# Windowed attention, an MLP and a routed MLP in one kernel: transposes in another PSUM bank, a hundred matmuls over ones, one step of a weight conversion on another engine

## The chip, the cores and the metric

The kernel runs on one core of a Trainium2 chip. The metric is the device time of one execution in microseconds (us). Engines are named as the profile names them: PE (matrix multiplications), DVE (vector), ACT (scalar and activation functions), POOL (GpSimd), SP (whose queue issues the DMAs).

## What is computed

Three layers stand one behind the other. The inputs of the first two are in float64 or float32; the weights `w_in` and `w_out` of the second arrive as float64.

```python
# q, k, v: 4 x 8 heads x 576 x 64; window 128, causal, a linear bias per head
scores = q @ k.T / sqrt(64);  scores = where(mask, scores + bias, -1e9)
attn = softmax(scores);       x = (attn @ v)  as 2304 x 512
# MLP, 512 -> 2048 -> 512
h = x @ w_in;  x = (h - tanh(h)) @ w_out
# 8 experts, each token goes to one: cosine similarity, argmax, softmax gate
out[mask_e] = gate * (relu(x[mask_e] @ w1[e]) @ w2[e])
```

## The kernel before, in words

The 2304 rows are 18 blocks of 128. Attention of a block is done in four quarters of two heads (`quarter`). The MLP works on two blocks at a time in eight steps (`step`), 72 steps in all; a step multiplies two column blocks of `w_in` (L686, into `h`), forms h - tanh(h) on ACT (L691) and DVE (L694), splits it in a high and a low part (L699 on ACT, L703 on DVE, `gh` and `gl`) and multiplies by `w_out` (L710). The first 16 steps cover the first four blocks. Routing (`route`) and the experts come behind.

The two MLP matrices come as float64 pairs of 32-bit words and are turned into float32 pairs on the chip (`weight`), 16 pieces of `w_in` (`rawi`) and 16 of `w_out` (`rawo`), 512 KB each. Of each piece: the DMA (L298 or L300); the top three bits of the lower words (L325, on ACT); a scaled copy of the upper words (L307 on ACT or L309 on DVE, into one of three buffers `wst`); the sign merged in (L328, DVE); both merged (L331, DVE); the high part (L313, ACT or DVE); the low part (L317, mostly POOL). L328, L331 and L703 read two tiles of SBUF each.

The first four blocks take an early form of attention in float32. A quarter multiplies q and k of two heads (L456, `sc`), adds the bias and takes the extreme (L484, DVE), takes the exponential (L498, ACT, into `p` or `p32x`), transposes the exponentials on PE (L518), copies the transposes out (L524, ACT or DVE, into `ptf`) and multiplies by v (L535, into `of`). Each of the two heads has one tile `sc` in PSUM that holds the scores in its first half and the transposes of the exponentials in its second:

```python
self.scores = [self.psA.tile([128, 2, 2, 128], F32, tag=f"sc{n}", ...) for n in range(2)]
sc = v["sc"][jj] = self.scores[jj][:, 0]      # scores
t = self.scores[jj][:, 1]                     # transposes
```

A further bank, `misc`, serves small products: transposes of x for the MLP (L633), the router's products, the expert embeddings.

The order of all instructions is set by a planner (`Plan`): each task has the engines that may run it with a cost in us, a due time and the keys that it reads and writes; the planner places the task that can start earliest, the lower due time first, on the engine where it ends first. An engine then runs its list in that order, and an instruction whose input isn't there holds up all behind it on that engine. Moving one cost therefore moves many instructions.

Of the kernel before, what the change touches and what calls it, by code (L numbers as in the profile page):

```python
# [10 lines left out]
F32 = mybir.dt.float32  # L11
# [40 lines left out]
WRATE2 = 1.0  # L52
PAD = 8
# [109 lines left out]
class Builder:  # L163
# [15 lines left out]
    def setup(self):  # L179
# [35 lines left out]
        self.scores = [self.psA.tile([128, 2, 2, 128], F32, tag=f"sc{n}", name=f"sc{n}") for n in range(2)]  # L215
# [18 lines left out]

    def small(self):
        nc, i = self.nc, self.i
        nc.gpsimd.memset(self.ones, 1.0)
        nc.gpsimd.memset(self.half, 0.5)
        nc.gpsimd.memset(self.cum, 0.0)
        nc.gpsimd.memset(self.oh, 0.0)  # L240
        for j in range(self.NOV):
            nc.gpsimd.memset(self.thr[:, :, j:j + 1], float(128 * j))
# [43 lines left out]
    def weight(self, P, j, kind, f, due):  # L286
# [35 lines left out]
        if kind == "o" and 1 <= FT - f < NF:  # L322
            slots = [("kf", FT - f, 0), ("kf", FT - f, 1)]
        P.add({"SP": 1.46}, load, due - 2 - (EARLY if self.early() else 0), w=[raw, (raw, "L")] + slots)
        P.add({"ACT": 0.68}, lambda e: nc.scalar.activation(  # L325
            out=v["L"], in_=v["L"].bitcast(U32), func=AF.Copy, scale=7.499 * 2.0 ** -32), due, r=[raw], w=[(raw, "L")])
# [109 lines left out]
    def quarter(self, P, a, due):  # L436
# [13 lines left out]
        def scores(jj):  # L450
            sc = v["sc"][jj] = self.scores[jj][:, 0]
# [63 lines left out]
        def tr_pe(jj):  # L515
            t = self.scores[jj][:, 1]
            for x in range(W // 128):
                nc.tensor.transpose(t[:, x, :], v["p32"][:, jj * W + x * 128:jj * W + (x + 1) * 128], self.ident)  # L518

        def tr_out(e, jj):  # L520
            if jj == 0:
                v["pt"] = self.at.tile([128, 512], F32, tag=f"pt{a % 2}", name="ptf", bufs=1)
            t = self.scores[jj][:, 1].rearrange("p s t -> p (s t)")
            (nc.scalar.copy if e == "ACT" else nc.vector.tensor_copy)(  # L524
                out=v["pt"][:, jj * W:(jj + 1) * W], in_=t[:, 0:W])
# [55 lines left out]
        for jj in range(2):  # L581
            if early:
                P.add({"PE": 0.45 if one else 0.65}, lambda e, jj=jj: scores(jj), due,
# [582 lines left out]
    def build(self):  # L1166
# [10 lines left out]
        P.add({"POOL": 0.6}, lambda e: self.small(), 0, w=["small", "cum"])  # L1177
# [240 lines left out]
```

## Time and profile before

| | |
|---|---|
| Median of 3 runs (lowest, highest) | 847.39 us (847.25, 847.75) |
| The profiled execution | 849.56 us |
| Its span, first to last instruction | 847.8 us |
| Busy share PE, DVE, ACT, POOL | 96%, 67%, 52%, 30% |
| Instructions PE, DVE, ACT, POOL | 5244, 1500, 997, 246 |
| Granted TensorE clock, mean over the span | 0.996 |

The profiled execution is 1.76 us longer than its span and 2.17 us longer than the median of the runs. Busy shares are means over the whole; the change acts on the first 150 us, so the rows below are of stretches of that part. An engine is busy there while an instruction is executing, also when that instruction is held up inside by another engine. Idle times are put down to what ended last.

### The profile page before, as it was taken

To read this page: it belongs to the slowest core of one execution; us is meant where nothing else is said; L and a number is where in the kernel's file an instruction comes from. 1 tells how busy PE (TensorE), PEld (TensorE's weight loads), DVE (VectorE), ACT (ScalarE), POOL (GpSimd) and SP (SyncE) were. 2 spreads that over 40 slices of the span, in tenths; PEclk is the share of its full clock that TensorE was granted. 3 is DMA by queue.
4 is the path that set the end of the run, shared out by engine and by line. 5 is a ranking of instruction groups with operands and counts; after the bars stand their busy time and mean duration, and the time that the engine had idled before them with its cause. 6 is when DMAs were issued, how large, how long until landed. Compare 5 with 4: busy or idle time off the path is not lost.

```text
span 847.8 us, 15246 instructions
## 1 busy us (share of the span) xinstructions
PE 816.7 (96%) x5244; PEld 721.2 (85%) x5244; DVE 565.5 (67%) x1500; ACT 441.6 (52%) x997; POOL 252.1 (30%) x246
## 2 busy tenths in 40 slices
PE   6999999999999999999999999999999999999995
PEld 4677878988888899988998998989889899998994
DVE  4658999987778577777776775576366656666230
ACT  3759876665555355555554543464255545545120
POOL 1424676554424233324242240021110210111011
PEclk9999999999999999999999999999999999999998
DMA  8973325945334234433434312365266656555000
GB/s 299 334 268 121 109 94 160 270 107 130 96 82 135 40 82 106 87 87 91 99 83 102 80 41 48 125 212 162 84 198 216 216 166 189 193 163 174 20 27 30
DMA packets 109464, 112.88 MB, mean 133 GB/s; under 512 B 62901, under 2 KB 75189, under 8 KB 109248
## 3 DMA queue, kind: packets, MB, share of 16 engines
q1 hardware_dynamic: 106240, 102.35, 42.2%
q0 software_dynamic: 3136, 9.46, 3.0%
q8 instruction: 43, 0.70, 0.4%
q14 instruction: 45, 0.37, 0.1%
HBM read 87.12 MB, written 17.48 MB: 123 GB/s over the span
## 4 chain that ended last, share of the span: by engine, by line
PE 71%; DVE 11%; DMA 7%; issue 6%; ACT 2%; SPq 2%; POOL 1%; POOLq 0%; DVEq 0%; ACTq 0%
PE h L686 19%; PE acc L710 17%; PE he L1014 9%; PE y L1049 8%; PE o L546 3%; DMA pt<-ph 3%; PE sc L456 3%; PE sc L462 2%; DMA out<-yo,ix 2%; DVE wst L331 2%; PE y L1045 2%; PE misc L785 2%; PE of L535 2%; DVE rawo L328 1%; PE sc L518 1%
## 5 line engine op out<-in xcount | busy, mean ns | idle before, releaser
L686 PE MATMUL h<-xT,wi 128*128 128x256 f32 x1728 | 228.8, 287 | 0.0
L686 PEld LDWEIGHTS h<-xT,wi 128*128 128x128 f32 x1728 | 219.4, 193 | 6.4 <-issue 2.6
L710 PE MATMUL acc<-wo,gh 128*128 128x512 f32 x576 | 183.9, 400 | 0.0
L710 PE MATMUL acc<-wo,gl 128*128 128x512 f32 x288 | 112.9, 392 | 2.0 <-DVE gl L703 2.0
L710 PEld LDWEIGHTS acc<-wo,gh 128*128 128x128 f32 x576 | 99.7, 189 | 15.1 <-issue 0.7
L691 ACT ACTIVATE t<-h 128x512 f32<-128x512 f32 x72 | 43.1, 599 | 100.3 <-PE h L686 95.3
L1049 PE MATMUL y<-eo,ge 128*128 128x512 f32 x336 | 88.5, 399 | 0.0
L484 DVE CUSTOM_DVE_ANT_0 sc<-sc,bias 128x256 f32<-128x256 f32 (+1 forms) x144 | 52.7, 372 | 46.3 <-PE sc L462 29.4
L498 ACT ACTIVATE p<-sc,mx 128x256 f32<-128x256 f32 (+1 forms) x128 | 59.3, 464 | 34.1 <-DVE mx L484 26.0
L1074 POOL DMA_INDIRECT out<-yo,ix x24 | 23.4, 975 | 176.2 <-PE y L1045 61.0
L1049 PEld LDWEIGHTS y<-eo,ge 128*128 128x128 f32 x336 | 60.0, 188 | 9.7
L710 PEld LDWEIGHTS acc<-wo,gl 128*128 128x128 f32 x288 | 54.1, 188 | 15.1 <-DVE gl L703 2.9
L508 POOL TENSOR_TENSOR ph<-p,ph 128x512 f16<-128x512 f32 (+1 forms) x38 | 46.1, 1214 | 69.3 <-ACT ph L503 26.0
L703 DVE TENSOR_TENSOR gl<-t,gh 128x512 fp32r<-128x512 f32 x72 | 63.0, 876 | 4.6 <-ACT gh L699 4.4
L948 DVE TENSOR_TENSOR eo<-est,eo 128x512 fp32r<-128x512 f32 x60 | 45.0, 752 | 30.4 <-ACT eo L944 29.4
L1036 DVE SCALAR_TENSOR_TENSOR ge<-he,ge 128x256 fp32r<-128x256 f32 x104 | 29.9, 325 | 51.9 <-ACT ge L1030 51.9
L694 DVE TENSOR_TENSOR t<-h,t 128x512 f32<-128x512 f32 x72 | 49.5, 687 | 19.0 <-ACT t L691 19.0
L944 ACT CAST eo<-est 128x512 fp32r<-128x512 f32 x64 | 39.7, 620 | 40.1 <-PE y L1045 21.5
L1014 PE MATMUL he<-xT,ei 128*128 128x320 f32 x384 | 60.4, 309 | 0.0
L1014 PEld LDWEIGHTS he<-xT,ei 128*128 128x128 f32 x384 | 58.3, 188 | 2.3
L1030 ACT ACTIVATE ge<-he 128x320 fp32r<-128x320 f32 (+1 forms) x56 | 24.1, 430 | 67.5 <-PE he L1014 61.7
L1014 PE MATMUL he<-xA,ei 128*128 128x320 f32 (+1 forms) x384 | 59.0, 302 | 0.0
(181 smaller groups left out, 1425.6 us busy)
## 6 DMA issues: line engine op xcount, KB each, us to landing
est<-in_w SPq DMA_DIRECT2D x128, 256.0 KB, 2.9
rawi<-in_w_in SPq DMA_DIRECT2D x16, 512.0 KB, 6.6
rawo<-in_w_out SPq DMA_DIRECT2D x16, 512.0 KB, 7.3
stk<-in_k SPq DMA_DIRECT2D x30, 256.0 KB, 2.7
stq<-in_q SPq DMA_DIRECT2D x28, 256.0 KB, 2.8
bucket<-in_c_pad SPq DMA_DIRECT2D x8, 771.0 KB, 5.8
xe<-bucket SPq DMA_DIRECT2D x17, 257.0 KB, 3.5
vst<-in_v SPq DMA_DIRECT2D x30, 128.0 KB, 2.4
```

Source lines behind the costliest of these rows:

```text
L484: nc.vector.tensor_tensor_reduce(out=x, in0=x, in1=self.bias[:, h, c0:c1], scale=-0.125, scalar=mx[:, 1:2] if m else 3.0e38, op0=ALU.add, ...
L498: nc.scalar.activation(out=v["p32"][:, jj * W:(jj + 1) * W], in_=x, func=AF.Exp, scale=-1.0, bias=v["mx"][jj][:, 0:1], accum_out=self.sums ...
L508: self.eng(e).tensor_tensor(out=ph[:, 2 * W:4 * W], in0=v["p32"][:, 0:2 * W], in1=ph[:, 0:2 * W], op=ALU.subtract)
L686: nc.tensor.matmul(h3(v["h"], f2), lhsT=w[:, a, k, :], rhs=xT[c][:, :, k, :], start=(k == 0 and n == 0), stop=(k == KD - 1 and n == 2))
L691: nc.scalar.activation(out=v["t"], in_=v["h"].rearrange("p a b -> p (a b)"), func=AF.Tanh)
L694: nc.vector.tensor_tensor(out=v["t"], in0=v["h"].rearrange("p a b -> p (a b)"), in1=v["t"], op=ALU.subtract)
L703: self.eng(e).tensor_tensor(out=v["gl"], in0=v["t"], in1=v["gh"].bitcast(F32), op=ALU.subtract)
L710: nc.tensor.matmul(self.acc[g, t], lhsT=v[a][:, c0:c0 + 128], rhs=self.w["o", fs[f2]][:, c, :], start=(first and f2 == 0 and n == 0), stop ...
L944: nc.scalar.copy(out=t[:, 0, :], in_=v["x"])
L948: self.eng(eng).tensor_tensor(out=t[:, 1, :], in0=v["x"], in1=t[:, 0, :].bitcast(F32), op=ALU.subtract)
L1014: nc.tensor.matmul(h[:, 0:N], lhsT=w[:, a, c0:c0 + 128], rhs=xT()[b][:, k, 0:N], start=(k == 0 and n == 0), stop=(k == KD - 1 and n == 2))
L1049: nc.tensor.matmul(y[t], lhsT=gt(f, a)[:, (t - ts[0]) * 128:(t - ts[0] + 1) * 128], rhs=self.w["o", f0 + f][:, b, :], start=(f == 0 and n ...
```

## The change

Three edits. The exponentials of the early quarters are transposed into the bank `misc`, both heads at once, and copied out by one instruction instead of two; the score tiles keep only the scores. A hundred matmuls over a tile of ones (128x128 by 128x512, bfloat16, into the bank of `acc0`, read by nobody) are put into the plan with due time 0, nine with a cost of 0.43 us and the others with 0.215. The tile of ones is set first. The top bits of the lower words are formed by POOL (booked at 0.95 us) instead of ACT (0.68 us). The planner's costs for the early products of PE are lowered.

```diff
+NWARM = 100
-        self.scores = [self.psA.tile([128, 2, 2, 128], F32, tag=f"sc{n}", name=f"sc{n}") for n in range(2)]
+        self.scores = [self.psA.tile([128, 2, 128], F32, tag=f"sc{n}", name=f"sc{n}") for n in range(2)]
+    def warm(self, P):
+        nc = self.nc
+        at = {}
+        def mm(e):
+            if 0 not in at:
+                at[0] = self.psA.tile([128, 512], F32, tag="acc0", name="idle", bufs=1)
+            nc.tensor.matmul(at[0], lhsT=self.ones, rhs=self.ones.unsqueeze(1).to_broadcast([128, 4, 128]), start=True,
+                             stop=True)
+        for n in range(NWARM):
+            P.add({"PE": 0.43 if n < 9 else 0.215}, mm, 0, r=["ones"], w=[("acc", 0)])
...
-        P.add({"ACT": 0.68}, lambda e: nc.scalar.activation(
-            out=v["L"], in_=v["L"].bitcast(U32), func=AF.Copy, scale=7.499 * 2.0 ** -32), due, r=[raw], w=[(raw, "L")])
+        P.add({"POOL": 0.95}, lambda e: nc.gpsimd.tensor_scalar(
+            out=v["L"], in0=v["L"].bitcast(U32), scalar1=7.499 * 2.0 ** -32, scalar2=None, op0=ALU.mult), due, r=[raw],
+            w=[(raw, "L")])
...
-        def tr_pe(jj):
-            t = self.scores[jj][:, 1]
-            for x in range(W // 128):
-                nc.tensor.transpose(t[:, x, :], v["p32"][:, jj * W + x * 128:jj * W + (x + 1) * 128], self.ident)
+        def tr_pe(e):
+            v["tp"] = self.misc()
+            for x in range(2 * W // 128):
+                c = slice(x * 128, (x + 1) * 128)
+                nc.tensor.transpose(v["tp"][:, c], v["p32"][:, c], self.ident)
...
-                P.add({"PE": 0.45 if one else 0.65}, lambda e, jj=jj: scores(jj), due,
+                P.add({"PE": 0.3 if one else 0.42}, lambda e, jj=jj: scores(jj), due,
...
-            for jj in range(2):
-                P.add({"PE": 0.28 if one else 0.5}, lambda e, jj=jj: tr_pe(jj), due, r=["at", "con", ("p32", pb, jj)],
-                      w=[("tp", jj)])
-            for jj in range(2):
-                P.add({"ACT": 0.3, "DVE": 0.29} if one else {"ACT": 0.38, "DVE": 0.42}, lambda e, jj=jj: tr_out(e, jj),
...
-            P.add({"PE": 0.85 if one else 1.65}, pv_f, due,
+            P.add({"PE": 0.3 if one else 0.52}, tr_pe, due, r=["at", "con", ("p32", pb, 0), ("p32", pb, 1)], w=[("tp", a)],
+                  take="misc")
+            P.add({"ACT": 0.4, "DVE": 0.42} if one else {"ACT": 0.6, "DVE": 0.69}, tr_out, due, r=["at", ("tp", a)],
+                  w=[("pt", a % 2)], free="misc")
+            P.add({"PE": 0.45 if one else 0.9}, pv_f, due,
...
+        P.add({"POOL": 0.3}, lambda e: nc.gpsimd.memset(self.ones, 1.0), -30, w=["ones"])
+        self.warm(P)
```

What this does to the order on three engines. PE, at its start, before (`kf`, `qf` are k and q of the early blocks):

```order
L456 MATMUL sc_92<-kf_128,qf_126 128x128
L456 MATMUL sc_93<-kf_128,qf_126 128x128
L518 MATMUL sc_92<-con,p_160 128x128
L456 MATMUL sc_92<-kf_128,qf_126 128x128
L269 MATMUL misc<-con,ec 128x8 x4
L518 MATMUL sc_93<-con,p_160 128x128
L456 MATMUL sc_93<-kf_128,qf_126 128x128
```

and now, behind the first pair of scores:

```order
L471 MATMUL sc_92<-kf_131,qf_128 128x128
L244 LDWEIGHTS ones
L244 MATMUL idle<-ones 128x512
L283 MATMUL misc<-con,ec 128x8 x4
L471 MATMUL sc_93<-kf_131,qf_128 128x128
...
L534 MATMUL misc<-con,p_175 128x128 x2
L471 MATMUL sc_92<-kf_131,qf_128 128x128
```

Nine of the matmuls over ones stand ahead of the first scores and all hundred ahead of the first product of the MLP; behind it there is none. Of the 32 early score products 24 stand ahead of it now, 21 before.

DVE, in the early attention of block 1, with what each instruction waits for; before (L484 is the bias, L553 and L554 the sums' reciprocals):

```order
L484 ISA sc_92,mx_376<-sc_92,bias 128x256 [waits Activation_49]
L484 ISA mx_376 128x1
L331 SCALAR_TENSOR_TENSOR wst<-wst,rawo_275 128x512 [waits DVE_49]
L484 ISA sc_93,mx_391<-sc_93,bias 128x256 [waits Activation_49]
L484 ISA mx_391 128x1
L313 CAST wo_394<-wst 128x512 [waits DVE_49]
L328 SCALAR_TENSOR_TENSOR rawo_298<-rawo_298 128x512 [waits DMAHW1_49]
L553 TENSOR_SCALAR sm<-sm 128x4 [waits Activation_49]
```

and now:

```order
L343 SCALAR_TENSOR_TENSOR rawo_334<-rawo_334 128x512 [waits DMAHW0_49,Pool_49]
L343 SCALAR_TENSOR_TENSOR rawo_354<-rawo_354 128x512 [waits DMAHW1_49,Pool_49]
L566 TENSOR_SCALAR sm<-sm 128x4 [waits Activation_49]
L567 RECIPROCAL sm<-sm 128x4 [waits DVE_49]
L499 ISA sc_92,mx_470<-sc_92,bias 128x256 [waits PE_49]
L499 ISA mx_470 128x1
L499 ISA sc_93,mx_480<-sc_93,bias 128x256 [waits PE_49]
L499 ISA mx_480 128x1
L346 SCALAR_TENSOR_TENSOR wst<-wst,rawo_334 128x512
```

The bias instruction waited for ACT (its copy of the transposes out of the same tile) and now waits for the scores alone; the sign merge (L328, now L343) waits for POOL as well.

POOL, behind its constants, before:

```order
L362 TENSOR_TENSOR khl<-stk,khl 64x512 x2
L317 TENSOR_TENSOR wi_283<-wst,wi_283 128x512
L429 TENSOR_TENSOR vst_272<-vst_272,vt 128x256
L317 TENSOR_TENSOR wi_329<-wst_88,wi_329 128x512
L433 TENSOR_TENSOR vt<-vst_272,vt 128x4x64
L317 TENSOR_TENSOR wo_394<-wst,wo_394 128x512
```

and now:

```order
L339 TENSOR_SCALAR rawi_233<-rawi_233 128x512
L339 TENSOR_SCALAR rawi_247<-rawi_247 128x512
L339 TENSOR_SCALAR rawi_274<-rawi_274 128x512
L377 TENSOR_TENSOR khl<-stk,khl 64x512
L339 TENSOR_SCALAR rawi_294<-rawi_294 128x512
L444 TENSOR_TENSOR vst_318<-vst_318,vt 128x256
L339 TENSOR_SCALAR rawo_334<-rawo_334 128x512
```

The 32 new instructions (L339) lead on POOL: 7 of them stand ahead of the first low part (L317, now L331), 20 ahead of the eighth, 31 ahead of the sixteenth. Up to DVE's subtraction (L694, now L705) of the twelfth step DVE loses five high parts (L313), four scalings (L309), six copies of transposes (L524), two bias pairs and a few small ones to ACT or to a later place, and takes one `khl`.

## Rows read from the trace of the kernel before

**Rows 1.** Busy time by stretch: us, busy (x instructions) of each engine, PEclk, DMA share, GB/s.
```profile
0.00:20.00 20.00, 13.51 (x44) 9.10 (x44) 9.38 (x43) 7.34 (x23) 3.33 (x27) 1.00 0.89 295
20.00:66.00 46.00, 45.00 (x159) 32.75 (x158) 28.36 (x73) 30.11 (x80) 14.10 (x13) 1.00 0.86 305
66.00:90.10 24.10, 22.90 (x146) 17.78 (x146) 21.98 (x43) 20.39 (x51) 12.53 (x8) 1.00 0.34 112
90.10:150.10 60.00, 53.95 (x352) 48.11 (x352) 57.62 (x89) 44.71 (x88) 41.92 (x29) 1.00 0.41 128
150.10:847.80 697.70, 681.40 (x4549) 613.50 (x4547) 448.13 (x1256) 339.07 (x758) 180.19 (x171) 1.00 0.43 118
```

**Rows 2.** Timeline of PE: start us, us, line, operation, tiles, count [idle before].
```profile
5.46 0.80 PE L456 MATMUL sc<-kf,qf 64*128 64x128 f32 x4 [5.46 <-DMA kf<-in_k]
...
30.63 1.97 PE L535 MATMUL of<-vf,ptf 128*128 128x64 f32 x8 [0.58 <-DVE ptf L524]
...
50.08 2.93 PE L686 MATMUL h<-xT,wi 128*128 128x256 f32 x12
...
67.51 1.71 PE L686 MATMUL h<-xT,wi 128*128 128x256 f32 x12
69.06 1.00 PE L535 MATMUL of<-vf,ptf 128*128 128x64 f32 x8
...
88.38 0.62 PE L710 MATMUL acc<-wo,gh 128*128 128x512 f32 x2
88.84 0.40 PE L710 MATMUL acc<-wo,gl 128*128 128x512 f32 x1
89.07 0.62 PE L710 MATMUL acc<-wo,gh 128*128 128x512 f32 x2
```

**Rows 3.** Waits of DVE, 0 to 66 us: us in total, times, longest.
```profile
DVE sc L484 <- ACT ptf L524: 11.2, 11, 2.4
DVE ptf L524 <- PE sc L456: 5.8, 4, 1.9
```

**Rows 4.** Timeline of DVE, 108 to 113 us, and its twelfth L694.
```profile
108.44 0.68 DVE L331 SCALAR_TENSOR_TENSOR wst<-wst,rawi 128x512 int32<-128x512 int32 x1
...
110.69 1.79 DVE L331 SCALAR_TENSOR_TENSOR wst<-wst,rawo 128x512 int32<-128x512 int32 x1
112.40 1.78 DVE L703 TENSOR_TENSOR gl<-t,gh 128x512 fp32r<-128x512 f32 x1
...
150.12 0.69 DVE L694 TENSOR_TENSOR t<-h,t 128x512 f32<-128x512 f32 x1
```

**Rows 5.** Timeline of POOL over the same stretch.
```profile
110.18 3.46 POOL L317 TENSOR_TENSOR wi<-wst,wi 128x512 fp32r<-128x512 f32 x2
```

**Rows 6.** Groups of DVE by form, 66 to 150.1 us: busy us, mean ns | idle before.
```profile
L331 DVE SCALAR_TENSOR_TENSOR wst<-wst,rawo 128x512 int32<-128x512 int32 x13 | 14.6, 1128 | 0.0
L328 DVE SCALAR_TENSOR_TENSOR rawo<-rawo 128x512 int32<-128x512 int32 x12 | 13.1, 1110 | 0.0
L703 DVE TENSOR_TENSOR gl<-t,gh 128x512 fp32r<-128x512 f32 x10 | 12.0, 1204 | 0.0
L328 DVE SCALAR_TENSOR_TENSOR rawi<-rawi 128x512 int32<-128x512 int32 x9 | 9.8, 1101 | 0.0
L331 DVE SCALAR_TENSOR_TENSOR wst<-wst,rawi 128x512 int32<-128x512 int32 x11 | 8.8, 796 | 0.0
```

**Rows 7.** Groups of DVE by form, 0 to 66 us.
```profile
L328 DVE SCALAR_TENSOR_TENSOR rawo<-rawo 128x512 int32<-128x512 int32 x4 | 3.5, 872 | 0.0
L313 DVE CAST wi<-wst 128x512 fp32r<-128x512 f32 x2 | 1.5, 741 | 0.0
L524 DVE COPY ptf<-sc 128x128 f32<-128x128 f32 x4 | 1.2, 291 | 2.5 <-PE sc L456 2.2 <-ACT p32x L498 0.3
L313 DVE CAST wo<-wst 128x512 fp32r<-128x512 f32 x2 | 0.8, 418 | 0.0
```

**Rows 8.** The pieces of w_in, top bits on ACT: duration ns min/median/max, first and last start.
```profile
L325 ACT ACTIVATE rawi<-rawi x16: 649/680/717, 16.5 to 95.4; 128x512 int32<-128x512 uint32 x16
```

More of the change, by code (lines that the diff above doesn't have):

```diff
@@ L233, in consts @@
               r=[("xr", 0)], w=["tri"])
+    def warm(self, P):
[8 more added lines that the diff above has]
+            P.add({"PE": 0.43 if n < 9 else 0.215}, mm, 0, r=["ones"], w=[("acc", 0)])
     def small(self):
         nc, i = self.nc, self.i
-        nc.gpsimd.memset(self.ones, 1.0)
         nc.gpsimd.memset(self.half, 0.5)
@@ L450, in scores @@
         def scores(jj):
-            sc = v["sc"][jj] = self.scores[jj][:, 0]
+            sc = v["sc"][jj] = self.scores[jj]
             j = qq + 2 * jj
@@ L513, in tr, with tr_out @@
             nc.sync.dma_start_transpose(out=v["pt"][:, 0:4 * W // 128, :], in_=v["ph"][:, 0:4 * W])
-        def tr_pe(jj):
-            t = self.scores[jj][:, 1]
-            for x in range(W // 128):
-                nc.tensor.transpose(t[:, x, :], v["p32"][:, jj * W + x * 128:jj * W + (x + 1) * 128], self.ident)
[L520 to L525, printed above, removed]
+        def tr_pe(e):
[3 more added lines that the diff above has]
+                nc.tensor.transpose(v["tp"][:, c], v["p32"][:, c], self.ident)
+        def tr_out(e):
+            v["pt"] = self.at.tile([128, 512], F32, tag=f"pt{a % 2}", name="ptf", bufs=1)
+            (nc.scalar.copy if e == "ACT" else nc.vector.tensor_copy)(out=v["pt"][:, 0:2 * W], in_=v["tp"][:, 0:2 * W])
         def pv_f(e):
@@ L596, in quarter @@
         if early:
-            for jj in range(2):
-                P.add({"PE": 0.28 if one else 0.5}, lambda e, jj=jj: tr_pe(jj), due, r=["at", "con", ("p32", pb, jj)],
-                      w=[("tp", jj)])
-            for jj in range(2):
-                P.add({"ACT": 0.3, "DVE": 0.29} if one else {"ACT": 0.38, "DVE": 0.42}, lambda e, jj=jj: tr_out(e, jj),
-                      due, r=["at", ("tp", jj)], w=[("pt", a % 2, 1)] if jj else [("pt", a % 2), ("pt", a % 2, 1)])
-            P.add({"PE": 0.85 if one else 1.65}, pv_f, due,
-                  r=["at", ("pt", a % 2), ("pt", a % 2, 1)] + [("vf", x) for x in ([b] if one else [b - 1, b])], w=[("o", qq)] if qq else ["o", ("o", 0), ("o", 1)])
+            P.add({"PE": 0.3 if one else 0.52}, tr_pe, due, r=["at", "con", ("p32", pb, 0), ("p32", pb, 1)], w=[("tp", a)],
[3 more added lines that the diff above has]
+            P.add({"PE": 0.45 if one else 0.9}, pv_f, due,
+                  r=["at", ("pt", a % 2)] + [("vf", x) for x in ([b] if one else [b - 1, b])], w=[("o", qq)] if qq else ["o", ("o", 0), ("o", 1)])
             if qq:
@@ L1176, in build @@
         P = Plan()
-        P.add({"POOL": 0.6}, lambda e: self.small(), 0, w=["small", "cum"])
+        P.add({"POOL": 0.3}, lambda e: nc.gpsimd.memset(self.ones, 1.0), -30, w=["ones"])
+        self.warm(P)
+        P.add({"POOL": 0.6}, lambda e: self.small(), 0, r=["ones"], w=["small", "cum"])
         self.consts(P)
```

## The prediction, with its working

> **What bounds the kernel now.** I read the stretches first [rows 1]. From 150.1 us to the end PE is busy 681 of 698 us: whatever the first 150 us gain is kept there, and nothing in the change touches that part. So the question is how early the kernel reaches the state of 150.1 us, for which I take DVE's subtraction of the twelfth MLP step, at 150.12 us [rows 4]. The first 150 us fall in two. Up to 66 us PE is busy nearly throughout and DVE in 9.38 of 20 and 28.36 of 46 us; then DVE is busy in 21.98 of 24.1 and 57.62 of 60 us while PE idles 7.2 us in all [rows 1].
>
> The second view is PE's timeline [rows 2]. The same twelve matmuls of the MLP take 2.93 us at 50.08 and 1.71 at 67.51, the same eight of the attention 1.97 at 30.63 and 1.00 at 69.06. PE runs at 1.2 GHz up to about 66 us, although it is hardly ever idle, and at 2.4 GHz behind. The column of the granted clock says 1.00 for both stretches [rows 1] and doesn't tell the levels apart; the durations do.
>
> The third is DVE's waits up to 66 us [rows 3]: 11.2 us for ACT's copy of the transposes out of the score tile and 5.8 for the same copies on DVE itself behind PE. The fourth sets DVE beside POOL [rows 4, 5]: an L331 takes 0.68 us alone, and 1.79 while POOL is in two of its two-operand instructions, the L703 behind it 1.78. The two don't run beside each other; DVE stands until POOL is through, 1.1 us.
>
> **PE's account.** The attention and the first MLP products occupy PE for 13.51 + 45.00 = 58.5 us at the low clock [rows 1], half of it, 29.2, if the clock were high throughout; the first few us can't be, so I count 27. The 7.2 us of idle time behind 66 us could go too. Against that stand the hundred matmuls. At the high clock a 512-column product starts every 0.23 us (three between 88.38 and 89.07) [rows 2], at the low one I estimate twice that, 0.46. The nine ahead of the first scores take 4.1 us of the 5.46 that PE waits there anyway [rows 2]: nothing. The other 91 cost 20.9 us, all ahead of the first MLP product, where PE has no room otherwise if they come as planned: 44.6 us from 5.46 to 50.08 [rows 2] become some 22 + 21 = 43, so that product starts hardly earlier, but with three more score products done and at the high clock. PE's account thus gives at most 27 + 7.2 - 20.9 = 13.3 us.
>
> **DVE's account up to the twelfth subtraction.** First, what leaves: five L313 and four L309 at about 0.42 [rows 7], L309 taken alike, are 3.8 us, six copies 2.0 (0.29 to 0.42 each) [rows 7], two bias pairs about 1.0, and the small ones (a cast of ph, a reduction, four fills) about 1.6; with the 0.5 that two of the casts lost to POOL this makes 8.9. One `khl` is added, below 0.5 and left out.
>
> Second, POOL's 32 new instructions. None is in the trace. They are off DVE and cost it only where they hold up its two-operand instructions. From 66 to 150.1 us these stand above 0.68 us by 13 x 0.45 (L331 on rawo), 11 x 0.12 (on rawi), 12 x 0.43 and 9 x 0.42 (L328) and 10 x 0.52 (L703) [rows 6]: 21.3 us over POOL's 8 + 29 instructions [rows 1], 0.58 us each, where DVE is full. Up to 66 us the same excess is about 1.8 us (four L328 at 872 ns, two L313 at 741) [rows 7] over 14 such instructions of POOL: 0.13 each, where DVE has gaps. Twenty of the new ones stand ahead of POOL's eighth low part, which lay before 66 us, twelve behind it. That gives 20 x 0.13 + 12 x 0.58 = 9.6. DVE will have fewer gaps than now, so I take 12. The lower end is 5, if one operand keeps POOL half as long; the upper is 32 x 0.58 = 18.6.
>
> Third, DVE's idle time, 10.6 + 17.6 + 2.1 + 2.4 = 32.8 us now [rows 1]. The first 10.6 stay, since the first piece of w_in is there at 16.5 us in either case [rows 8]. Of the 17.6 the waits for the copies in the score tile go, DVE's own copies go with them [rows 3], and the scores come at the high clock, though spread by the matmuls over ones; I keep 7. Behind 66 us POOL's longer queue (a low part waits behind top bits, which wait for a DMA) lets me keep 3.4 of 4.5. Idle time falls to 21, by 11.8.
>
> The sum is -8.9 + 12 - 11.8 = **-8.7 us**, below PE's bound of 13.3, so DVE's account decides. ACT loses 32 instructions of 0.68 us [rows 8] and ten copies; it is busy in 65 of the 84 us behind 66 [rows 1] and holds nobody up for long, so that counts nothing by itself. Its freed time is what the nine casts and scalings use. The `misc` bank is held for one pair of transposes and one copy at a time, about 1.2 us per quarter against some 3.6 us per quarter on PE (43 us for twelve): covered. SP's order keeps its pieces, with four instead of two of w_in's near the end; they wait for slots of the early attention, which comes free earlier. 849.56 - 8.7 = 840.9 for the profiled execution, which stands 2.17 above the median: **838.7 us** in the median.
>
> **A rule that speaks against it.** The rows say that an L331 beside POOL takes 1.79 instead of 0.68 us [rows 4, 5]. The Trainium skill ("SBUF — State Buffer", section "Who interferes with whom") states it as an exclusive lock: a DVE instruction with two SBUF inputs and a GpSimd one exclude each other, and the second waits until the first is through. The trace agrees with its 1.1 us. By that rule alone, without gaps, each new POOL instruction could cost DVE its whole length, which is the slower rival below. The Trainium skill also says ("GPSIMD Engine Reference", section "4.1 Engine selection") that one-input operations run at about line rate there and two-input ones about twice as long; by it the second term would be nearer 5 and the result 832, which no row here shows.
>
> **The rivals.**
> *DVE stops being the bound (chance 0.18).* If the new POOL instructions are short and DVE's gaps close further, PE's account decides: 13.3 us less, 834.1. For it: the waits of [rows 3] lie just where PE was slow. Against: DVE's 57.62 of 60 us.
>
> *Nothing comes of it (0.10).* PE waits for DVE wherever it is faster, with the gaps before 66 us kept, because the matmuls over ones stretch a quarter to the old 3.6 us and so pace DVE as before. Then the idle term falls to about 0, and -8.9 + 9.6 is no change: 847 to 849.
>
> *POOL locks DVE out (0.08).* The wait per new instruction is that of the L703 beside POOL, 1.1 us [rows 4]. The second term is 32 x 1.1 = 35, the sum -8.9 + 35 - 11.8 = +14.5: 862. It turns to the slower side above (8.9 + 11.8) / 32 = 0.65 us per instruction, little more than the 0.58 that full stretches show. Against: 20 of the 32 stand where DVE has gaps.
>
> *The clock doesn't rise (0.05).* The change then does not do what it is for: the attention has kept PE busy for 58 us without the high clock coming. With short products between them the hundred might not do either, or the clock might fall again. The 91 then cost 41.9 us, the first MLP product starts at about 90 us, and the work that PE does now from 50.08 to 150.12 (100 us) follows in 85, without its 7.2 us of idle time and 8 us of the low clock: +25, 872. Against it: the clock rose at about 66 us, behind runs of twelve MLP products such as that at 50.08 [rows 2], and the products over ones are, like those, on full 128x128 weights. The Trainium skill ("TensorE: Matmul & The Clock Gate", section "What's actually happening") says that the throttled state is the default and activity releases it; this trace agrees for those MLP products and not for the 58 us of attention.
>
> **How the numbers follow.** The forecast has 0.58, the rivals 0.18, 0.10, 0.08 and 0.05; 0.01 is left for the unknown. The forecast's own range is from its second term: 5 gives 831.7, bounded by PE at 834.1, and 18.6 gives 845.3. The range for eight in ten takes in the first rival with some 2 us below it and the lower part of "nothing comes of it": 832 to 848. Within 0.2% (1.7 us, about what a measurement of this kernel can tell from no change) is the second rival, less a little on each side: 0.09. Faster: 0.58 + 0.18 and that little, 0.77. Slower: 0.08 + 0.05 and the rest, 0.14.
>
> **What the new profile would show.** Right: twelve MLP products at 1.7 us from the first on, attention products at half their old durations from about 8 us; the bias instruction on DVE waiting for scores alone; the excess of DVE's two-operand instructions grown by about 12 us up to the twelfth subtraction, and that one at 141 us instead of 150.1; new POOL instructions of 0.6 to 1.2 us; PE idle below 10 us between the first MLP product and 141 us. Wrong: products still at the low clock between 10 and 50 us; DVE idle in 20 to 50 us as before; L328 and L331 at 1.3 us or more on average; a stretch of waits on PE behind its first MLP product as long as what it saved.

## The result and the profile after

| | before | after |
|---|---|---|
| Median of 4 runs each on one chip (lowest, highest) | 847.57 us (847.25, 848.44) | 857.25 us (855.12, 858.0) |
| Ratio, 95% interval | | 1.0122 [1.0099, 1.0146] |
| Profiled execution, span | 849.56, 847.8 us | 858.0, 856.3 us |

The change makes the kernel 1.2% slower; 1.0% faster was forecast. Busy time by stretch after the change, with the cuts and columns of [rows 1]:

```profile
0.00:20.00 20.00, 17.98 (x88) 9.56 (x88) 10.50 (x43) 9.43 (x29) 6.07 (x29) 1.00 0.90 305
20.00:66.00 46.00, 40.47 (x237) 26.17 (x236) 30.12 (x67) 25.36 (x63) 43.22 (x30) 1.00 0.90 314
66.00:90.10 24.10, 20.50 (x114) 15.11 (x113) 16.39 (x36) 15.01 (x39) 22.96 (x17) 0.98 0.27 88
90.10:150.10 60.00, 56.72 (x364) 50.21 (x362) 54.84 (x80) 38.84 (x73) 48.16 (x32) 0.98 0.36 118
150.10:856.30 706.20, 684.46 (x4552) 615.60 (x4550) 452.67 (x1266) 339.12 (x760) 186.28 (x175) 0.99 0.43 118
```

POOL's column is the one that changed: 43.22 of 46 and 22.96 of 24.1 us, where it had 14.10 and 12.53 [rows 1]. From 20 to 90 us it is the busiest engine. Its two largest groups from 0 to 110 us (busy us, mean ns):

```profile
L339 POOL TENSOR_SCALAR rawo<-rawo 128x512 int32<-128x512 uint32 x16 | 28.0, 1751 | 1.8 <-DMA rawo<-in_w_out 0.6
L339 POOL TENSOR_SCALAR rawi<-rawi 128x512 int32<-128x512 uint32 x16 | 27.1, 1695 | 9.8 <-DMA rawi<-in_w_in 8.6
```

One of them in the view of the tile `rawi` after the change (duration ns min/median/max, first and last start):

```profile
L339 POOL TENSOR_SCALAR rawi<-rawi x16: 1549/1585/2076, 15.8 to 106.2; 128x512 int32<-128x512 uint32 x16
```

And the waits after the change, 0 to 110 us, those of ACT for POOL (us in total, times, longest):

```profile
ACT wst L321 <- POOL wi L331: 11.8, 6, 4.1
ACT wst L321 <- POOL wo L331: 9.8, 7, 2.9
...
ACT vt L446 <- POOL vst L444: 6.6, 3, 3.0
```

The 32 new instructions take 55.1 us of POOL. The planner had them at 0.95 us each, the prediction expected 0.6 to 1.2; none took less than 1.55. The low parts (L331) stand behind them in POOL's list, each holds one of the three buffers `wst`, and ACT's next scaling (L321) waits for that buffer 21.6 us. The chain of a weight thus runs at POOL's pace, ACT's freed time is spent waiting, and DVE gets its work late.

PE's timeline after the change (columns as in [rows 2]), at the start, at the first MLP products and at the 17th step:

```profile
1.11 3.48 PE L244 MATMUL idle<-ones 128*128 128x512 bf16 x9 [1.11 <-POOL half L252]
5.50 0.49 PE L471 MATMUL sc<-kf,qf 64*128 64x128 f32 x4 [0.91 <-DMA kf<-in_k]
...
31.52 1.00 PE L548 MATMUL of<-vf,ptf 128*128 128x64 f32 x8
...
60.60 3.21 PE L697 MATMUL h<-xT,wi 128*128 128x256 f32 x24
...
192.52 0.28 PE L697 MATMUL h<-xT,wi 128*128 128x256 f32 x1
194.74 4.51 PE L697 MATMUL h<-xT,wi 128*128 128x256 f32 x23 [1.94 <-DVE xT L657]
```

The high clock is there by 5.50 us: four score products take 0.49 us where they took 0.80 at 5.46, and eight attention products take 1.00 us at 31.52, where they took 1.97 at 30.63 [rows 2]. Yet the first MLP product starts at 60.60 us, 10.5 later than at 50.08 [rows 2]. At 194.74 PE has waited 1.94 us, and 23 products take 4.51 us, where 24 took 3.21 at 60.60: behind the wait PE is at 1.2 GHz again for a while. Here the granted clock shows it, with a mean of 0.63 from 194 to 198 us (columns as in [rows 1]):

```profile
194.00:198.00 4.00, 3.26 (x16) 3.26 (x17) 1.80 (x5) 0.57 (x2) 0.00 (x0) 0.63 1.29 254
```

To see where time goes I follow DVE's subtractions of the 72 MLP steps (L694 before, L705 after, as in [rows 4]), each against the same step before. The twelfth is at 150.06 us, so -0.1:

```profile
150.06 0.69 DVE L705 TENSOR_TENSOR t<-h,t 128x512 f32<-128x512 f32 x1
```

The 16th is at +1.5, the 17th at +8.9, the 36th at +6.2, the 72nd at +9.0. So the distance from the forecast has two parts: the 8.7 us that the first twelve steps were to gain did not come, and 7.4 us were lost in one step, the 17th. It is the first step of token blocks 4 and 5, whose attention, alone among those so far, goes through the transposing DMAs.

### The profile page after: what moved, and what is told of

The parts are those of the page before. It is cut to its first block, busy times and chain, and to the rows that moved or that the text cites. A ratio compares the mean times of both kernels' runs of the same rounds, so it can differ in the third digit from the quotient of the medians.

```text
span 856.3 us, 15453 instructions
## 1 busy us (share of the span) xinstructions
PE 820.1 (96%) x5344; PEld 716.7 (84%) x5344; DVE 564.5 (66%) x1486; ACT 427.8 (50%) x962; POOL 306.7 (36%) x279
## 4 chain that ended last, share of the span: by engine, by line
PE 62%; DMA 11%; POOL 9%; DVE 8%; issue 7%; ACT 2%; SPq 1%; POOLq 0%; DVEq 0%; ACTq 0%
PE h L697 16%; PE acc L721 14%; PE he L1025 10%; PE y L1060 8%; DMA pt<-ph 6%; PE o L559 3%; DMA out<-yo,ix 3%; POOL rawo L339 2%; PE y L1056 2%; PE sc L477 2%; POOL rawi L339 2%; PE misc L796 1%; POOL wo L331 1%; DVE wst L346 1%; POOL ph L523 1%
## 5 line engine op out<-in xcount | busy, mean ns | idle before, releaser
L697 PE MATMUL h<-xT,wi 128*128 128x256 f32 x1728 | 226.3, 285 | 3.5 <-DVE xT L657 1.9
L1060 PE MATMUL y<-eo,ge 128*128 128x512 f32 x336 | 88.5, 399 | 0.0
L714 DVE TENSOR_TENSOR gl<-t,gh 128x512 fp32r<-128x512 f32 x72 | 65.7, 913 | 13.2 <-ACT gh L710 13.0
L523 POOL TENSOR_TENSOR ph<-p,ph 128x512 f16<-128x512 f32 (+1 forms) x35 | 43.6, 1246 | 66.4 <-ACT ph L518 30.5
L705 DVE TENSOR_TENSOR t<-h,t 128x512 f32<-128x512 f32 x72 | 49.5, 687 | 18.0 <-ACT t L702 18.0
L1041 ACT ACTIVATE ge<-he 128x320 fp32r<-128x320 f32 (+1 forms) x56 | 24.1, 430 | 69.4 <-PE he L1025 64.0
```

The lines of the kernel that those rows point to most:

```text
L523: self.eng(e).tensor_tensor(out=ph[:, 2 * W:4 * W], in0=v["p32"][:, 0:2 * W], in1=ph[:, 0:2 * W], op=ALU.subtract)
L697: nc.tensor.matmul(h3(v["h"], f2), lhsT=w[:, a, k, :], rhs=xT[c][:, :, k, :], start=(k == 0 and n == 0), stop=(k == KD - 1 and n == 2))
L705: nc.vector.tensor_tensor(out=v["t"], in0=v["h"].rearrange("p a b -> p (a b)"), in1=v["t"], op=ALU.subtract)
L714: self.eng(e).tensor_tensor(out=v["gl"], in0=v["t"], in1=v["gh"].bitcast(F32), op=ALU.subtract)
L1060: nc.tensor.matmul(y[t], lhsT=gt(f, a)[:, (t - ts[0]) * 128:(t - ts[0] + 1) * 128], rhs=self.w["o", f0 + f][:, b, :], start=(f == 0 and n ...
```

## The experiments

In every row the columns "12th" to "72nd" are the start of that subtraction in the profiled execution minus its start before (150.12, 183.09, 191.71, 329.15 and 581.29 us). A median is compared only with the one of before in its own row; the ratio is the number to read for the time. The columns show where the time goes, in one execution of each kernel, and that execution is not always a typical one: before it took 849.56 us (medians 845.83 to 848.14), in e2 867.09 (864.07), in e12 856.48 (852.23), in e11 847.34, the fastest of four runs that reach up to 862.44. The change and e6, and e3 and e5, run the same instructions up to some 174 us and differ by 0.9 to 2.3 us at the twelfth and the 16th step. Smaller differences in these columns say nothing.

| | median, before (us) | ratio, 95% interval | 12th | 16th | 17th | 36th | 72nd |
|---|---|---|---|---|---|---|---|
| the change | 857.25, 847.57 | 1.0122 [1.0099, 1.0146] | -0.1 | +1.5 | +8.9 | +6.2 | +9.0 |
| e1_act | 846.66, 845.92 | 1.0000 [0.9986, 1.0015] | -8.9 | -7.5 | -2.2 | -3.4 | -1.1 |
| e2_pool_only | 864.07, 845.92 | 1.0213 [1.0188, 1.0238] | +18.6 | +18.1 | +16.2 | +18.0 | +17.9 |
| e3_half | 843.78, 845.92 | 0.9978 [0.9963, 0.9994] | -14.0 | -13.2 | -5.4 | -6.5 | -4.1 |
| e4_booked | 850.08, 845.92 | 1.0047 [1.0031, 1.0064] | +0.1 | +0.9 | -0.8 | +1.8 | +1.6 |
| e5_half_vt | 842.08, 847.14 | 0.9947 [0.9927, 0.9967] | -12.5 | -10.9 | -3.5 | -6.1 | -4.4 |
| e6_change_vt | 856.56, 847.14 | 1.0112 [1.0078, 1.0146] | -1.0 | -0.6 | +6.5 | +3.8 | +5.9 |
| e7_ones_only | 855.94, 847.14 | 1.0119 [1.0082, 1.0156] | +7.2 | +5.3 | +3.5 | +6.2 | +7.6 |
| e8_transposes_only | 848.33, 847.14 | 1.0016 [0.9986, 1.0045] | -5.5 | -5.8 | +3.8 | +0.3 | -0.9 |
| e9_half_lead1 | 843.85, 845.83 | 0.9970 [0.9951, 0.9989] | -10.7 | -11.4 | -9.7 | -7.5 | -4.6 |
| e10_half_lead2 | 842.63, 845.83 | 0.9952 [0.9935, 0.9970] | -10.5 | -9.1 | -11.3 | -8.7 | -5.8 |
| e11_half_lead4 | 852.72, 845.83 | 1.0118 [1.0047, 1.0190] | -0.8 | -5.6 | -7.7 | -3.3 | -1.8 |
| e12_before_lead2 | 852.23, 845.83 | 1.0076 [1.0051, 1.0100] | +7.6 | +7.7 | +6.3 | +8.3 | +7.4 |
| e13_change_lead2 | 855.09, 847.66 | 1.0104 [1.0074, 1.0134] | +1.0 | +3.0 | +0.8 | +3.6 | +5.4 |
| e14_act_lead2 | 846.42, 847.66 | 0.9991 [0.9973, 1.0009] | -1.5 | -4.6 | -6.1 | -3.9 | -2.5 |
| e15_either_lead2 | 843.38, 847.66 | 0.9970 [0.9950, 0.9990] | -10.9 | -11.2 | -12.4 | -6.9 | -6.2 |
| e16_quarter_lead2 | 839.75, 847.66 | 0.9916 [0.9886, 0.9947] | -13.7 | -11.9 | -14.1 | -11.8 | -9.1 |
| e17_quarter | 842.61, 848.14 | 0.9934 [0.9912, 0.9956] | -15.1 | -14.2 | -6.4 | -9.1 | -6.6 |
| e18_quarter_lead2_no_ones | 840.11, 848.14 | 0.9921 [0.9896, 0.9946] | -4.3 | -8.5 | -8.7 | -7.8 | -9.3 |

### Whose time POOL's new instructions cost

Three theories of the first part. *Occupancy*: POOL's own time is the bound. *Port*: POOL's instructions hold DVE up. *Order*: the plan, made with POOL at 0.95 us, is poor. **e1_act** takes the third edit back:

```diff
-        P.add({"POOL": 0.95}, lambda e: nc.gpsimd.tensor_scalar(
-            out=v["L"], in0=v["L"].bitcast(U32), scalar1=7.499 * 2.0 ** -32, scalar2=None, op0=ALU.mult), ...
+        P.add({"ACT": 0.68}, lambda e: nc.scalar.activation(
+            out=v["L"], in_=v["L"].bitcast(U32), func=AF.Copy, scale=7.499 * 2.0 ** -32), ...
```

> The change with the top bits back on ACT, all else kept (transposes in misc, the hundred matmuls). Occupancy theory (POOL is the bound from 20 to 110 us, because each new instruction takes 1.6 to 1.7 us and the low parts and the splits of k and q queue behind it): POOL busy below 70% in every 10 us up to 110, first MLP product at 50 us or earlier, 832 to 842 us. Matmuls theory (the hundred matmuls ahead of the first MLP product delay it): that product at 55 us or later and 850 us or more.

**e2_pool_only** makes the same edit the other way round, alone, in the kernel before.

> The kernel before with the top bits on POOL and nothing else. Occupancy theory: slower than before, 855 to 870 us, POOL busy above 90% from 20 to 110 us. Matmuls theory: the step alone is harmless, 845 to 850 us. Port theory (DVE held up by POOL): slower too, but then with the sign merge and the merge on DVE at 1.2 us or more on average; occupancy theory has them at about 0.9 to 1.1, as in the change.

**e3_half** keeps the change's plan and gives POOL half the columns, ACT the other half:

```diff
+        def top(e):
+            lo, up = v["L"][:, 0:256], v["L"][:, 256:512]
+            nc.gpsimd.tensor_scalar(out=lo, in0=lo.bitcast(U32), ...)
+            nc.scalar.activation(out=up, in_=up.bitcast(U32), ...)
+        P.add({"POOL": 0.95}, top, ...)
```

> The change with the same plan and order, but each top-bits instruction split: POOL does 256 of the 512 columns, ACT the other 256 at the same place of its list. Occupancy theory: POOL's part takes 0.8 to 0.9 us, POOL is relieved of some 27 us, 838 to 848 us. Matmuls theory: nothing changes, 855 to 858. Order theory (the plan books 0.95 us and is wrong by 0.7): with POOL's part near the booked time the order fits again, so 835 to 845, and the planner's booking of 1.6 in the next run does the same.

**e4_booked** only tells the planner the price: `P.add({"POOL": 1.6}, ...)` for 0.95.

> The change with POOL's top bits booked at 1.6 us instead of 0.95: the same work in an order that knows their length. Order theory: 838 to 846 us. Occupancy theory: POOL stays above 90% busy up to 110 us, whatever the order, 850 to 860 us.

The top bits on POOL alone cost 2.1% (e2), and without them the rest of the change is at the time of before (e1: 846.66 us, between the ranges of its two theories; its first MLP product starts at 53.2 us). With half the columns, in the change's own plan, the twelfth subtraction comes 14.0 us earlier than in the change (e3). POOL is still over 90% busy from 30 to 100 us there; what comes earlier is the work behind the new instructions: the 16th of the 32 low parts starts at 87.9 us in e3 and at 88.5 in e1, at 101.0 in the change and at 95.6 before. Booking the true price (e4) wins nothing at the twelfth step, though this is no clean test of the order, since the new plan gives DVE more to do (busy 125.0 us up to there, 111.8 in the change). But e4 loses nothing in the 17th step, and by its ratio it is 0.47% slower than before where the change is 1.22%. So occupancy decides the twelfth step; at the end the order weighs as much. For the port, first DVE's timeline in the change, 47 to 53 us:

```profile
47.81 0.69 DVE L346 SCALAR_TENSOR_TENSOR wst<-wst,rawi 128x512 int32<-128x512 int32 x1 [1.84 <-ACT wst L321]
...
50.42 0.69 DVE L343 SCALAR_TENSOR_TENSOR rawo<-rawo 128x512 int32<-128x512 int32 x1
51.75 0.69 DVE L346 SCALAR_TENSOR_TENSOR wst<-wst,rawo 128x512 int32<-128x512 int32 x1
52.35 0.69 DVE L343 SCALAR_TENSOR_TENSOR rawo<-rawo 128x512 int32<-128x512 int32 x1
```

and POOL's over the same stretch:

```profile
47.17 3.22 POOL L339 TENSOR_SCALAR rawi<-rawi 128x512 int32<-128x512 uint32 x2
50.48 3.98 POOL L339 TENSOR_SCALAR rawo<-rawo 128x512 int32<-128x512 uint32 x2
```

In this stretch DVE's two-operand instructions keep their 0.69 us beside L339, and POOL's pair is the one that grows, 3.98 for 3.22 us. In others DVE does wait for a part of an L339. DVE's timeline at 88 us:

```profile
88.07 1.13 DVE L346 SCALAR_TENSOR_TENSOR wst<-wst,rawi 128x512 int32<-128x512 int32 x1
...
89.74 1.14 DVE L346 SCALAR_TENSOR_TENSOR wst<-wst,rawi 128x512 int32<-128x512 int32 x1
```

and POOL's:

```profile
87.65 3.61 POOL L339 TENSOR_SCALAR rawo<-rawo 128x512 int32<-128x512 uint32 x2
```

Of the 24 instructions L343, L346 and L714 up to 150 us that meet L339 and nothing else on POOL, 14 take 0.68 to 0.69 us and ten 0.80 to 1.15; none waits for the whole of an L339. DVE's groups by form, 66 to 150.1 us after the change:

```profile
L343 DVE SCALAR_TENSOR_TENSOR rawo<-rawo 128x512 int32<-128x512 int32 x12 | 13.4, 1136 | 0.0
L346 DVE SCALAR_TENSOR_TENSOR wst<-wst,rawo 128x512 int32<-128x512 int32 x12 | 13.3, 1105 | 1.9 <-ACT wst L321 1.9
L714 DVE TENSOR_TENSOR gl<-t,gh 128x512 fp32r<-128x512 f32 x11 | 12.1, 1103 | 7.8 <-ACT gh L710 7.7
L346 DVE SCALAR_TENSOR_TENSOR wst<-wst,rawi 128x512 int32<-128x512 int32 x10 | 9.6, 957 | 0.0
...
L343 DVE SCALAR_TENSOR_TENSOR rawi<-rawi 128x512 int32<-128x512 int32 x6 | 7.4, 1260 | 0.0
```

1136, 1105 and 1103 ns stand where 1110, 1128 and 1204 stood, 957 and 1260 where 796 and 1101 stood [rows 6]. The time of all five above 0.68 us is 21.5 us, where it was 21.3; with the part up to 66 us it grows from 22.4 to 25.3 us. Hold-ups count as busy time, and the loss isn't there: up to the twelfth subtraction DVE is busy 111.8 us in the change and 114.2 in e1, and idle 38.3 and 27.0. The port theory falls as the cause; some 3 us of DVE's time are what it explains.

### The other two edits

**e7_ones_only** puts `self.warm(P)` with its tile of ones into the kernel before.

> The kernel before with the hundred matmuls over ones alone: its exponentials go through the DMA as before and ACT keeps the top bits. DVE's account: DVE is the engine that bounds the first 110 us and loses no work here, so a faster clock buys little: 844 to 848 us. PE's account: the cold products of the first 40 us cost more than the fillers, and the time is 836 to 842 us. The fillers run in front of products that are due: 850 us or more.

**e8_transposes_only** is e1_act without `self.warm(P)`.

> The change without matmuls over ones and with the top bits back on ACT: the early exponentials go through PE's transposes into the small products' bank, on a cold PE in the first 40 us. DVE's account: 8.9 us of DVE's work are gone whatever the clock, so the 12th subtraction comes 5 to 9 us early as in e1_act, and the end at 844 to 848 us. PE's account: the transposes and the single float products at half clock add what the 27 us of the prediction's sum say, and the time is 852 us or more.

The fillers (the hundred matmuls) alone cost 1.2%, the worst of the three expectations. (In this kernel the early exponentials go through PE, L518, and not through the DMA as that text says.) The first MLP product starts at 67.0 us (50.08 before), and DVE is busy 131.2 us up to the twelfth subtraction, 13.8 more than before; by what chain was not followed. The transposes alone come out like e1, at the time of before (e8's runs lie between 842.21 and 852.63 us), though both are 5 to 9 us ahead at the twelfth step. Both lose that lead again: e8 9.6 us in the 17th step, e1 5.3 us there.

### The 17th step

In the change and in e3 one instruction stands out at that place. DVE's timeline in the change:

```profile
189.26 3.39 DVE L448 TENSOR_TENSOR vt<-vst,vt 128x256 bf16<-128x256 f32 x1
...
194.00 0.69 DVE L657 TENSOR_TENSOR xT<-misc,xT 128x512 fp32r<-128x512 f32 x1
```

and POOL's beside it:

```profile
189.38 0.63 POOL L585 TENSOR_TENSOR xr<-xr,sm 128x256 f32<-128x256 f32 x1
189.96 1.28 POOL L385 TENSOR_TENSOR qst<-stq,qst 128x512 fp32r<-128x512 f32 x1
191.20 1.16 POOL L523 TENSOR_TENSOR ph<-p,ph 128x512 f16<-128x512 f32 x1
```

DVE stands 3 us beside three of POOL's two-operand instructions, and the residual's split (L657), for which PE waits, comes behind. I took this meeting for the cause. **e5_half_vt** and **e6_change_vt** give that one instruction to POOL, in e3's kernel and in the change:

```diff
+        def low(e):
+            if e == "DVE" and not self.moved:
+                self.moved, e = True, "POOL"
+            self.eng(e).tensor_tensor(out=v[2], in0=st["v"], in1=v[1], op=ALU.subtract)
```

> The kernel of e3_half with one instruction on another engine, in the same place of the program: the first lower part of v that DVE subtracts (128x256, 3.39 us at 174.75 us in e3_half, where DVE's thirteen others take a median of 0.42) goes to POOL. Lockout theory: that one instruction stands still while POOL runs three two-operand instructions end to end (174.88 to 177.85); behind it wait the residual's split for the next products (PE idle 1.95 us) and on SP the load into its buffer with two transposing DMAs behind it (PE idle 1.86 us), and after these pauses 60 products run at half clock: 7 to 8 us in all. Without it step 17 keeps the 13 us gained at step 16, and the time is 836 to 838.5 us. Order theory: the later blocks' attention lags by the plan, whoever subtracts this part; the waits come back some microseconds later, and the time is 842 to 845 us.

> The change itself with that same one instruction on POOL (3.39 us at 189.26 us there). Lockout theory: the loss between the 16th and the 17th subtraction (+1.5 to +8.9 us against the kernel before) goes, and the time is 848.5 to 851 us. Order theory: 856 to 858 us. If POOL's load of the first 110 us and this one meeting are the whole loss, this and e3_half add up: change minus 14 minus 7.

Both miss: the 17th step still loses 7.4 and 7.1 us. What took the place of the 3.39 us, in DVE's timeline of e5:

```profile
177.96 2.92 DVE L575 TENSOR_SCALAR sm<-sm 128x4 f32<-128x4 f32 x1 [0.32 <-POOL xr L594]
```

and in POOL's:

```profile
177.25 0.63 POOL L594 TENSOR_TENSOR xr<-xr,sm 128x256 f32<-128x256 f32 x1
177.82 0.68 POOL L456 TENSOR_TENSOR vt<-vst,vt 128x256 bf16<-128x256 f32 x1
178.45 1.28 POOL L388 TENSOR_TENSOR qst<-stq,qst 128x512 fp32r<-128x512 f32 x1
179.70 1.15 POOL L532 TENSOR_TENSOR ph<-p,ph 128x512 f16<-128x512 f32 x1
```

Now an instruction over 128x4 numbers stands until POOL's run ends at 180.85 us. So moving one instruction leaves DVE's stop where it was. Why is this step late in most of these kernels? The attention of blocks 4 and 5 gets its due times from the plan. PE's first product of it with v, before:

```profile
139.41 0.73 PE L546 MATMUL o<-vt,pt 128*128 128x192 bf16 x8
```

and in the change:

```profile
149.48 0.73 PE L559 MATMUL o<-vt,pt 128*128 128x192 bf16 x8
```

In e1 it starts at 138.3 and in e3 at 135.5 us: 1.1 and 3.9 us earlier than before, where the MLP's products are 9 and 14 us ahead. (This is not the first product of that attention, as the expectation of e9 has it: single scores stand earlier, from 113.3 us before, 100.3 in the change, 82.1 in e1 and 87.9 in e3.) **e9**, **e10** and **e11** have it due 1, 2 and 4 steps earlier in e3's kernel, **e12** 2 steps earlier in the kernel before, **e13** in the change:

```diff
-                d0 = p - 8 * rate - LEAD + 4 * n * rate
+                d0 = p - 8 * rate - (LEAD + 2 if g == 2 else LEAD) + 4 * n * rate
```

> The kernel of e3_half with the attention of token blocks 4 and 5 (the first that goes through the transposing DMAs, and the first products of which are step 17) due one step earlier in the plan. Second-bound theory: in every kernel so far the 17th subtraction stands at 186 to 201 us, 7 to 18 us behind the 16th where the first half was faster, since the planned attention of these blocks begins at 135 to 149 us whatever the products gained; due a step (some 7 us) earlier, PE waits less for the residual there and the time is 838 to 841 us. Total-work theory: VectorE and the other engines have no room for it before, the products of steps 9 to 16 come later by as much, and the time stays at 842.5 to 845 us.

> The same, due two steps earlier. Second-bound theory: no wait is left at step 17, 13 us gained there stay to the end but for a few: 836 to 839 us. Total-work theory: 842 to 846 us.

> The same, due four steps earlier. Second-bound theory: no better than two steps, since the wait at step 17 is gone by then, and the attention now stands in front of weights that the first twelve steps need: 838 to 844 us. Total-work theory: 846 us or more.

> The kernel before with the attention of blocks 4 and 5 due two steps earlier: a control. Second-bound theory: PE waits under 1 us between steps 16 and 17 of the kernel before, so there is nothing to win: 845 to 849 us, and what e10_half_lead2 wins over e3_half comes from the change. If it wins as much here as there, the plan was poor in itself and the change has nothing to do with that part.

> The change itself with the attention of blocks 4 and 5 due two steps earlier. Second-bound theory: the loss between steps 16 and 17 (+1.5 to +8.9 us) goes and POOL's load up to step 12 stays: 849 to 852 us. POOL theory for that loss too (POOL's backlog from the top bits delays the splits that this attention needs, so that a due time changes nothing): 856 to 860 us.

In e9 1.7 us of the loss in the 17th step are left, in the others with an earlier due time none: e13 stands at +0.8 behind +3.0, where the change has +8.9 behind +1.5. PE's timeline there, in e13:

```profile
188.83 3.03 PE L697 MATMUL h<-xT,wi 128*128 128x256 f32 x24
```

The 24 products come without a wait and at the high clock. That the late attention is the cause of this step's loss is shown. The end moves less: against e3, e9 and e10 keep 0.5 and 1.7 us of it at the 72nd subtraction, against the change e13 keeps 3.6, and the intervals of the ratios overlap in both comparisons. Steps 9 to 16 pay a part (e10 has -9.1 at the 16th, e3 -13.2), four steps are too many (e11), and in the kernel before the same edit costs 0.8%, all of it by the twelfth step (e12, which misses its 845 to 849 us). Second bound is right about the 17th step; the times of e9, e10 and e11 lie where total work had them, and that of e13, 855.09 us, between its two ranges.

### What is left of the change

**e14_act_lead2** is e1_act with that due time, **e15_either_lead2** the change with it and `P.add({"ACT": 0.68, "POOL": 1.6}, top, ...)`, **e16_quarter_lead2** is e10 with columns 0 to 127 on POOL and the others on ACT, **e17_quarter** is e16 with the old due time, **e18_quarter_lead2_no_ones** is e16 without `self.warm(P)`.

> The change with its top bits on ACT (e1_act) and the same attention two steps earlier. If the prediction failed only in POOL's price and in taking the gain of the first 150 us for kept, this is the kernel that it forecast: 838 to 842 us. If ACT's 0.68 us for each of the 64 (the part that the prediction took for free on ACT) or DVE's load before step 12 bounds it, 844 to 848 us.

> The change with the planner free to give each of the top bits' instructions to ACT at 0.68 or to POOL at 1.6 us, and the attention two steps earlier. Occupancy theory: some go to POOL where it idles, and neither engine is the bound: 838 to 842 us. If it does no better than e10_half_lead2 (842.6), the choice by instruction is worth nothing over the split by columns.

> The kernel of e10_half_lead2 with 128 of the 512 columns on POOL and 384 on ACT. Occupancy theory: POOL's 32 instructions are shorter still (1.08 us at 256 columns), ACT's longer; if POOL still bounds the first 66 us, 840 to 842 us; if ACT, whose part runs beside it, has become the bound, 843 to 845 us.

> The change with 128 of 512 columns on POOL and 384 on ACT, its attention due as in the change. Both bounds matter: a little better than e3_half (0.9978) and worse than e16 (0.9916): ratio 0.994 to 0.997, with a loss of 5 us or more between steps 16 and 17. If the due time is worth nothing, the ratio is 0.990 to 0.993.

> The kernel of e16 without the hundred matmuls over ones. PE's account: the transposes and single float products run at half clock until PE's clock rises by itself, and the first 60 us lose more than the ones took: ratio 0.997 to 1.003. DVE's account: DVE and the weights' arrival set the first 66 us, the ones are worth nothing: ratio 0.990 to 0.994.

e14 misses the forecast's range and lies in the other, 844 to 848 us (the top bits are 32 instructions, not the 64 of that text): its twelfth step is at -1.5, and DVE is busy in 57.33 of the 60 us from 90.1 (busy time by stretch, columns as in [rows 1]):

```profile
90.10:150.10 60.00, 55.85 (x375) 49.68 (x374) 57.33 (x102) 44.25 (x93) 41.42 (x29) 1.00 0.50 128
```

With the top bits on ACT, DVE is nearly full there as it was before, and earlier attention takes room from the weights. e15, where the planner puts 19 of the 32 on POOL, does no better than e10 (0.9970, 0.9952): a choice by instruction is worth nothing over the split by columns. e16 is the fastest kernel here, 0.8% below before and, by the two ratios, 2% below the change. e17 lies between e3 and e16, with 7.8 us lost in the 17th step where e16 loses none: the intervals of e16 and e17 overlap, so what the due time gives at the end is not settled. POOL's groups in e16 for its quarter (busy us, mean ns):

```profile
L341 POOL TENSOR_SCALAR rawo<-rawo 128x128 int32<-128x128 uint32 x16 | 11.9, 747 | 4.3 <-DMA rawo<-in_w_out 3.2
L341 POOL TENSOR_SCALAR rawi<-rawi 128x128 int32<-128x128 uint32 x16 | 10.9, 684 | 13.0 <-DMA rawi<-in_w_in 12.0
```

e18 says that the hundred matmuls give nothing that can be measured at the end. PE's timeline in e18:

```profile
45.35 2.88 PE L700 MATMUL h<-xT,wi 128*128 128x256 f32 x12
48.05 1.01 PE L551 MATMUL of<-vf,ptf 128*128 128x64 f32 x8
```

Without them the first MLP product starts at 45.35 us (54.74 in e16), and behind one group of twelve the clock is high by itself (1.01 us for eight attention products). e16 is 9.4 us ahead of e18 at the twelfth step, level with it at the 72nd: that lead is lost in the later steps. What takes it there is only in part named: PE's waits for transposing DMAs from 210 to 640 us are 6.9 us in e16 (below: us in total, times, longest) and 4.1 before. That they are the cause was not tried.

```profile
PE o L562 <- DMA pt<-ph: 6.9, 10, 1.4
```

## Why the prediction was wrong

- **The clock**: right. It is high by 5.50 us and the attention runs at half its old durations. The sign given for it, full 128x128 weights, was none: the attention's L535 has 128*128 too [rows 2] and ran at the low clock.
- **"POOL's 32 new instructions ... are off DVE and cost it only where they hold up its two-operand instructions"**: this step failed, and it decides the sign. The term of 12 us for holding up measured some 3 us (the groups above: 25.3 us over 0.68 where 22.4 stood), below its lower end of 5. (In its working the two groups named up to 66 us make 1.4 us, not 1.8; that changes nothing.) What they cost was POOL's own 55.1 us and what queues behind it. The rows had it: a two-operand low part took 1.73 us on POOL [rows 5], so that 32 would take 55 us at that length; the new instructions lead its list, 31 of them ahead of the sixteenth low part, and POOL's own time was never summed. No rival had POOL as the bound; the one called "POOL locks DVE out" has the right sign and a mechanism that the runs exclude as the cause.
- **"Behind 66 us POOL's longer queue ... lets me keep 3.4 of 4.5"**, and of DVE's idle time 21 us in all: measured up to the twelfth subtraction are 9.5 + 15.9 + 7.7 + 5.2 = 38.3, more than the 32.8 before. DVE's busy time fell by 5.5 us, its idle time rose by as much.
- **"ACT loses 32 instructions ... that counts nothing by itself"**: right, ACT gives the time back as waits for `wst`.
- **"The sum is -8.7 us"**: the change is at -0.1. e1, without POOL's load, is at -8.9. That is luck in the terms: DVE is busy 114.23 of its 141.25 us, 3.1 less than before, and idle 27.0, 5.8 less, where 8.9 (with no hold-up) and 11.8 were forecast.
- **"Whatever the first 150 us gain is kept there"**: this failed too. In the profiled executions e1 keeps 1.1 of 8.9 us and e3 4.1 of 14.0; by its ratio of 1.0000 e1 keeps nothing. That PE is busy 681 of 698 us says how little it waits when the first part takes as long as it did; a faster first part runs into an attention of blocks 4 and 5 that comes hardly earlier. What takes the lead in the later blocks stays open. The twelfth subtraction describes the MLP alone, and not where the attention of the next blocks stands.
- **"PE's account"**: its bound of 13.3 us was reached and perhaps passed: e3, e16 and e17 are 13.7 to 15.1 us ahead at the twelfth step, e5, the same program as e3 up to there, 12.5. Its view that the matmuls over ones hardly pay holds at the end (e16 against e18).
- **The rule on the port.** The Trainium skill ("SBUF — State Buffer", "Who interferes with whom") says that a two-operand instruction of DVE contends with a GpSimd one that reads SBUF, under an exclusive lock. Beside the one-input L339 the trace agrees in part: ten of 24 of DVE's wait, up to 0.47 us, none for the 1.55 us or more that an L339 takes, and in one stretch POOL's are the ones that grow, 1.99 instead of 1.61 us each. The page also lists `tensor_scalar` among those that can contend when their operands meet its conditions, and e5's 2.92 us for 128x4 numbers agree.
- **The rule on the price.** The Trainium skill says ("GPSIMD Engine Reference", "4.1 Engine selection") that one-input operations run at about line rate on GpSimd. The trace disagrees for this one: 1549 ns at least, against 680 on ACT [rows 8] and 1261 or more for the two-operand low part on POOL (tile `wst` after the change, ns min/median/max):

```profile
L331 POOL TENSOR_TENSOR wi<-wst,wi x15: 1261/1301/1744, 32.0 to 139.5; 128x512 fp32r<-128x512 f32 x15
```

## What to carry to other kernels

When work moves to an idle engine, make that engine's account first: its own time for the new instructions, estimated at first by the longest like instruction in its rows, and what stands behind them in its list and holds buffers. A gain in an early stage can be lost where the next stage's other inputs are no earlier; follow a landmark for each of the streams that meet, here products and attention. Split by columns and not by instruction, a small share of the work on the slow engine can be right where all of it is wrong.

## What the hardware showed unexpectedly

- POOL's conversion of unsigned 32-bit words has a fixed part: a mean of 0.72 us at 128 columns (e16), 1.08 at 256 (e3), 1.72 at 512 (the change), from which I estimate some 0.4 us and 2.5 to 2.8 ns a column.
- A run of three of POOL's two-operand instructions can hold DVE until the run ends, and not for one of them only: 3.39 us in the change and in e3, 2.92 in e5, the latter for a 128x4 instruction of one input that takes 0.16 us elsewhere. It need not: in [rows 4, 5] DVE came in between two of POOL's. What makes the difference was not tried.
- The high clock, once there, falls again behind a wait of 1.94 us: 23 products take 4.51 us in the change, at a mean granted clock of 0.63 from 194 to 198 us.
